# Laying the feature map's weights out once, so that the fusing products read contiguous columns

## The chip, the cores and the metric

The kernel runs on one core of a Trainium2 chip. The metric is the device time of one execution in microseconds (us). Three executions of the kernel before took 780.72, 781.41 and 781.92 us; their median is 781.41 us.

## What is computed

Two attention branches share the input x (2048 tokens of 512 values) and are mixed by a gate. Branch A is softmax attention, branch B is linear attention with a learned feature map. Both have 32 heads of 16 values. Cut to what matters:

```python
# A
q, k, v = split_heads(x @ A_wqkv)
a = softmax(q @ k.T * 16 ** -0.5) @ v                 # per head
a = merge_heads(a) @ A_wo
# B
q, k, v = split_heads(x @ B_wqkv)
pq, pk = q @ w_phi[h], k @ w_phi[h]                   # per head, 16 x 16
phi = lambda p: concat(softmax(p), softmax(-p))
kv, z = phi(pk).T @ v, phi(pk).sum(tokens)
b = merge_heads((phi(pq) @ kv) / (phi(pq) @ z + 1e-6)) @ B_wo
g = sigmoid((x * gate_w).sum(-1))
out = g * a + (1 - g) * b
```

## The kernel before

**Branch A** fills most of the span. It runs over 4 chunks of 512 queries, 8 groups of heads in each, and 16 tiles of 128 keys, with 4 heads of a group side by side in the TensorE array. `_scores` (L993) multiplies kT and qT for one head: 32 rows of the array, 128 columns, 512 queries. ScalarE takes most of the scores, two banks of PSUM at a time, and writes their exponentials to ET (`_exp`, L1041). VectorE takes the others (L900, L925) and builds approximate exponentials from integer bits in the tiles vs and va. `_values` (L1100) multiplies the exponentials with V or with its scaled copy V2, on 32 columns of the array per head. V2 is written by GpSimd, one copy for each pair of key tiles (L805). `_norm` divides by the sums.

**Branch B** is threaded through the same time. `_b_fuse` (L1205 to L1224) folds the feature map into the projection: WT holds the transposed B_wqkv for the keys (s=1) or the queries (s=0), and the products of WT with w_phi (L1216) give new projection weights, which VectorE copies to WB (L1221). There are 4 column chunks of WT by 4 groups of 8 heads for each s, so 32 products of 128 x 128 by 128 columns; four of them share a bank of PSUM. For each group of 8 heads, the tile wphi holds a 128 x 128 matrix that is zero but for eight 16 x 16 blocks on its diagonal. Its columns stand in the order of heads and, in each head, of features. The rest of branch B wants the order (group of four heads, feature, head in the group), so each product reads its moving operand through a rearranged view:

```python
ins = e.matmul(self._bank(job)[:, P * cp:P * cp + P], self.WT[:, cp, P * c:P * c + P],
               self.wphi[:, cp, :].rearrange("p (g i f) -> p g f i", g=2, i=4), start=True, stop=True)
```

The fused weights are used in `_b_pair`, the values in `_b_v`, and the two meet in `_b_kv` (L1356) and `_b_num` (L1406). The gate's products with x are computed by TensorE too, between the two rounds of fusing.

**Loads.** `_consts` sets wphi to zero on GpSimd (L611) and loads w_phi into it with eight DMAs on SyncE's queue (L615). WT is loaded transposed (L1208), for s=1 early, for s=0 when the products of s=1 have been read.

**Order of the work.** All operations are recorded first with engine, estimated cost, buffers read and written, and a priority. `Plan.order` then picks one after another in simulated time and so fixes the order on each engine; `Plan.emit` writes the engines' instruction streams with waits on semaphores. On each engine, instructions run in that order. The recorded cost of four fusing products is 4 * c_pe(128), whatever the view.

Of the kernel before, what the change touches and what calls it, by code (L numbers as in the profile page):

```python
# [7 lines left out]
ALU = mybir.AluOpType  # L8
# [5 lines left out]
DH = 16  # L14
# [51 lines left out]
class Plan:  # L66
# [43 lines left out]
    def op(self, eng, fn, cost, reads=(), writes=(), deps=(), name="", prio=0.0, rel=-99, kind="full",  # L110
           acquire=None, release=None, lat=None, array=None, strips=None, also=None):
        o = Op(eng, fn, cost, name, prio, rel, kind, self.LAT[eng] if lat is None else lat)
        found = {}
        for b in reads:
            for w in b.writers:
                found[id(w)] = w
        for b in writes:
            for w in b.readers or b.writers:
                found[id(w)] = w
            if b.readers:  # L120
                for w in b.writers:
                    found[id(w)] = w
        for d in deps:
            if d is not None:
                found[id(d)] = d
        found.pop(id(o), None)
        o.deps = list(found.values())
        for b in reads:
            b.readers.append(o)
        for b in writes:  # L130
            b.writers, b.readers = [o], []
        o.acquire, o.release, o.also = acquire, release, also
        o.strips = strips
        o.port = eng == "POOL" or eng == "DVE" and name in self.PORT
        o.held = eng == "PE" and acquire is None and name in self.HOLDING
        o.array = cost if array is None else array
        self.ops.append(o)
        return o
# [257 lines left out]
class _Kernel:  # L396
# [183 lines left out]
    def _consts(self):  # L580
        op = self.plan.op
        B = Buf
        self.b_iden, self.b_mask = B(), B()
        self.b_V = [[B() for _ in range(self.NT // 2)] for _ in range(4)]
        self.b_V2 = [[B() for _ in range(self.NT // 2)] for _ in range(4)]
        self.early = {}
        self.b_VB = [B() for _ in range(4)]
        op("POOL", lambda e: e.memset(self.iden[:], 0.0), 0.25, writes=[self.b_iden], prio=-90)
        op("POOL", lambda e: e.affine_select(
            out=self.iden[:], in_=self.iden[:], pattern=[[-1, P]], compare_op=ALU.not_equal,  # L590
            fill=1.0, base=0, channel_multiplier=1), 0.3, reads=[self.b_iden], writes=[self.b_iden], prio=-89)
        for s in range(2):
            op("DVE", lambda e, s=s: e.tensor_reduce(
                self.mask[:, s:s + 1], self.iden[:].rearrange("p (i s d) -> p s i d", i=4, s=2)[:, s], AX.XY, ALU.add),
                0.3, reads=[self.b_iden], writes=[self.b_mask] if s else [B()], prio=-80)
        self.b_bm = B()
        op("DVE", lambda e: e.tensor_reduce(self.bm[:], self.iden[:].rearrange("p (v i) -> p i v", i=4), AX.X, ALU.add),
           0.3, reads=[self.b_iden], writes=[self.b_bm], prio=-20)
        n = 4 * self.NT * self.VCP
        self.o_vones = op("POOL", lambda e: e.memset(  # L600
            self.V[:, 0:n].rearrange("p (h v) -> p h v", v=17)[:, :, 16:17], 1.0), 1.0, prio=-70)
        self.o_vpad = op("POOL", lambda e: e.memset(self.V[:, n:], 0.0), 0.1, prio=-69)
        self.o_vbones = op("POOL", lambda e: e.memset(self.VB[:, :, :, 64:68], 1.0), 0.3, prio=-20)
        self.b_zero, self.b_warm = B(), B()
        op("DVE", lambda e: e.memset(self.warm[:], 1.0), 0.3, writes=[self.b_warm], prio=-95)
        op("POOL", lambda e: e.memset(self.zero[:], 0.0), 0.1, writes=[self.b_zero], prio=-75)
        self.b_guess = [B(), B(), B()]
        for t, b in zip((self.guess, self.guess_n, self.guess_b), self.b_guess):
            op("POOL", lambda e, t=t: e.memset(t[:], 0.0), 0.2, writes=[b], prio=-10)
        self.b_wphi0 = B()  # L610
        z = op("POOL", lambda e: e.memset(self.wphi[:], 0.0), 0.6, prio=-30)  # L611
        parts = []
        phi = self.B_w_phi.rearrange("(c h) d f -> h d c f", h=8)
        for hh in range(8):
            parts.append(lambda e, hh=hh: e.dma_start(self.wphi[16 * hh:16 * hh + 16, :, 16 * hh:16 * hh + 16], phi[hh]))  # L615
        self._shared_dma("wphi", parts, self.b_wphi, -5, [z])
        self.dma("SP", "wob", lambda e: e.dma_start(self.WoB[:], self.B_wo.rearrange("(q p) n -> p q n", p=P)),
                 writes=[self.b_WoB], prio=-3, lat=4.5)

# [539 lines left out]
    def _branch_b(self):  # L1159
        op, NT, NQC = self.plan.op, self.NT, self.NQC  # L1160
        B = Buf
        self.b_bq = [B() for _ in range(self.NBQ)]
        self.b_WT = B()
        self.b_WP = [B() for _ in range(2)]
        self.b_tree, self.b_bsum, self.b_brec = B(), B(), B()
        self.b_kv = [B() for _ in range(2)]
        self.b_kvbd, self.b_onB, self.b_rinvB = B(), [B(), B()], [B(), B()]
        self.b_numB, self.b_numR = [B(), B()], B()
        self.b_eps = [B() for _ in range(4)]
        self.b_phiT = [B() for _ in range(4)]  # L1170
        for x in self.b_phiT:
            x.readers = [r for s in (1, 2) for b in self.b_WA[s] for r in b.readers]
        self.b_onTB = [B() for _ in range(4)]
        self.outs = []
        self.n_pair = self.n_phit = 0
        z = op("POOL", lambda e: e.memset(self.kvbd[:], 0.0), 1.0, writes=[self.b_kvbd], prio=-10)
        for s in (1, 0):
            self._b_fuse(s, self.K0 - 10 + 5 * (1 - s))
        for b in self.b_onTB:
            b.readers = list(self.b_WT.readers)  # L1180
        for t in range(0, NT, 2):
            due = self.K0 + self.SK * t
            if self.RATIO:
                slot = self._b_pair(1, t, due)
                for k in range(2):
                    self._b_v(t + k, due + self.BV + k)
                self._b_kv(t, slot, due + self.BV + 7)
                continue
            self._b_v(t, due)
            self._b_v(t + 1, due + 1)  # L1190
            self._b_kv(t, self._b_pair(1, t, due), due + 12)
        self._b_kvbd(self.Q0 - 2)
        for ch in range(NQC):
            for tt in (0, 2):
                t = 4 * ch + tt
                due = self.Q0 + self.SQ * t
                phi = self._b_pair(0, t, due)
                for k in range(2):
                    self._b_phit(tt + k, phi, k, due + 12 + 2 * k)
                    self._b_num(t + k, self._num_due(t + k))  # L1200
                    self._b_out(tt + k)
# [4 lines left out]
    def _b_fuse(self, s, due):  # L1206
        op = self.plan.op
        self.dma("SP", f"wt{s}", lambda e: e.dma_start(self.WT[:], self.B_wqkv[:, D * s:D * s + D], transpose=True),  # L1208
                 writes=[self.b_WT], prio=-8 if s else due - 10, rel=-99 if s else due - 12, lat=5.0, cost=8.0 if s else 4.4)
        done = []  # L1210
        for c in range(4):
            job = Job()

            def mm(e, c=c, job=job):
                for cp in range(4):
                    ins = e.matmul(self._bank(job)[:, P * cp:P * cp + P], self.WT[:, cp, P * c:P * c + P],  # L1216
                                   self.wphi[:, cp, :].rearrange("p (g i f) -> p g f i", g=2, i=4), start=True, stop=True)
                return ins
            m = op("PE", mm, 4 * self.c_pe(128), reads=[self.b_WT, self.b_wphi], name="wphi", prio=due + 1,
                   acquire=job)  # L1220
            done.append(op("DVE", lambda e, c=c, job=job: e.tensor_copy(  # L1221
                self.WB[:, c, D * s:D * s + D], self._bank(job)), self.c_dve(512), deps=[m],
                name="wphi_ev", prio=due + 1, release=job))
        self.b_WP[s].writers = done  # L1224
# [329 lines left out]
```

## Time and profile before

| | |
|---|---|
| median of 3 executions | 781.41 us |
| profiled execution, time | 781.93 us |
| profiled execution, span | 780.1 us |
| busy: TensorE (PE), VectorE (DVE), ScalarE (ACT), GpSimd (POOL) | 754.9, 711.2, 753.0, 208.9 us |
| exponentials, L1041 on ACT | 785, 725.3 us |
| idle time of ACT before them | 13.4 us, 13.0 of it ended by the scores of L993 |
| fusing products, L1216 on PE | 32, 7.8 us, between 56.8 and 89.6 us |
| mean granted TensorE clock | 0.986 |

The profile shows one execution; its span lies within the time of the same execution. The engines are PE (matmul), PEld (loading of weights into the array), DVE, ACT and POOL. Line numbers are those of the kernel before. "Busy" on PE counts matmuls in flight, which overlap: a matmul's own duration is longer than the distance between the starts of two that follow each other. "<-" names what ended an idle time, and the clock column is the share of full speed that TensorE was granted.

### The profile page before, as it was taken

The page shows a single profiled execution, that of the slowest core. Times are in us where ns is not written, and L with a number is a line of the kernel's source. Part 1 is how long each engine was busy: PE and PEld are TensorE (multiplying, and loading weights), DVE is VectorE, ACT ScalarE, POOL GpSimd, SP SyncE. Part 2 cuts the span into 40 slices and gives each one's busy share as a digit, 9 for nine tenths or more (in the row PEclk, how much of TensorE's full clock was granted, in tenths as well). Part 3 has the DMA queues.
Part 4 walks back from the last instruction along what each step waited for, and adds up shares of the span by engine and source line. Part 5 has one row for each costly group of instructions (what it writes and reads, how often), then busy time and mean ns, then how long its engine had stood idle before and what let it go on. Part 6 is the DMA issues. An engine that isn't in the chain of part 4 may idle for free.

```text
span 780.1 us, 16892 instructions
## 1 busy us (share of the span) xinstructions
PE 754.9 (97%) x7047; PEld 218.5 (28%) x7111; DVE 711.2 (91%) x1158; ACT 753.0 (97%) x807; POOL 208.9 (27%) x300
## 2 busy tenths in 40 slices
PE   8999999999999999999999999999999999999998
PEld 3322223322222222222222222222222222222222
DVE  3864898899999999999998999999999999999994
ACT  6996899999999999999999999999999999999996
POOL 2210034601533234414234132130424231140000
PEclk9995999999999999999999999999999999999999
DMA  9501010000000000010111103112020312102010
GB/s 221 131 2 28 1 14 5 12 1 8 9 1 9 8 4 12 2 14 2 15 36 43 27 21 35 35 32 26 15 42 14 40 30 49 21 8 35 15 16 28
DMA packets 89180, 20.78 MB, mean 27 GB/s; under 512 B 83472, under 2 KB 88592, under 8 KB 89104
## 3 DMA queue, kind: packets, MB, share of 16 engines
q1 hardware_dynamic: 87232, 18.92, 13.5%
q8 instruction: 56, 0.92, 0.5%
q10 hardware_dynamic: 1872, 0.79, 0.4%
q14 instruction: 20, 0.16, 0.1%
HBM read 4.21 MB, written 2.10 MB: 8 GB/s over the span
## 4 chain that ended last, share of the span: by engine, by line
ACT 74%; PE 19%; DVE 5%; DMA 1%; issue 1%
ACT ET L1041 71%; PE ps L993 6%; PE ps L1100 5%; PE ps L677 4%; ACT bq L1283 3%; PE ps L788 2%; DVE vs L900 2%; DVE vs L925 1%; PE ps L1216 1%; DMA xT<-in_A_x_dram 1%; DVE bq L1256 0%; DVE btree L1277 0%; DVE ghB L841 0%; PE ps L685 0%; PE ps L724 0%
## 5 line engine op out<-in xcount | busy, mean ns | idle before, releaser
L1041 ACT ACTIVATE ET<-ps 128x1024 bf16<-128x1024 f32 (+1 forms) x785 | 725.3, 1165 | 13.4 <-PE ps L993 13.0
L900 DVE TENSOR_SCALAR vs<-ps 128x512 uint16<-128x512 f32 x482 | 312.5, 682 | 25.0 <-PE ps L993 23.5
L993 PE MATMUL ps<-qT,kT 32*128 32x512 bf16 (+1 forms) x2052 | 317.2, 387 | 10.9 <-ACT ET L1041 5.9
L925 DVE TENSOR_SCALAR vs<-vs 128x2048 uint16<-128x2048 uint16 (+2 forms) x242 | 233.8, 976 | 1.2
L1100 PE MATMUL ps<-vs,V 128*32 128x512 bf16 x1928 | 211.3, 385 | 0.6 <-DVE vs L925 0.3
L1100 PE MATMUL ps<-ET,V 128*32 128x512 bf16 x1566 | 196.6, 390 | 0.3 <-DVE vs L900 0.2
L993 PEld LDWEIGHTS ps<-qT,kT 32*128 32x128 bf16 x2052 | 77.7, 91 | 317.7 <-ACT ET L1041 291.5
L1286 POOL TENSOR_TENSOR btree<-btree 128x512 f16<-128x512 f16 (+1 forms) x32 | 37.7, 1180 | 187.5 <-DVE btree L1285 186.5
L1100 PEld LDWEIGHTS ps<-ET,V 128*32 128x32 bf16 x1566 | 49.1, 94 | 82.4 <-issue 73.5
L1107 PE MATMUL ps<-kT,zero 128*32 128x512 bf16 x664 | 66.5, 384 | 0.0
L1100 PEld LDWEIGHTS ps<-vs,V 128*32 128x32 bf16 x1928 | 48.2, 95 | 51.2 <-issue 31.1
L1274 POOL TENSOR_SCALAR bq<-bq 128x1024 bf16<-128x1024 bf16 x16 | 20.3, 1266 | 138.3 <-DVE bq L1256 94.5
L677 PE MATMUL ps<-WB,xT 128*128 128x512 bf16 x169 | 51.9, 383 | 2.7 <-issue 2.2
L1138 POOL TENSOR_TENSOR T<-T,rinv 128x512 bf16<-128x512 f32 x15 | 17.3, 1156 | 109.4 <-DVE rinv L1136 109.4
L767 POOL TENSOR_SCALAR qT<-qtmp,mask 128x512 bf16<-128x512 bf16 x30 | 25.8, 866 | 45.3 <-DVE qtmp L762 44.9
L677 PE MATMUL ps<-xT,WA 128*128 128x512 bf16 x95 | 32.9, 401 | 2.5 <-issue 1.6
L1121 DVE STREAM_TRANSPOSE T<-ps 128x512 f32<-128x512 f32 x32 | 22.7, 710 | 13.1 <-PE ps L1100 13.0
L1283 ACT ACTIVATE bq<-bq 128x2048 bf16<-128x2048 bf16 x16 | 32.9, 2056 | 0.0
L1256 DVE CAST bq<-ps 128x512 bf16<-128x512 f32 x32 | 21.7, 681 | 1.7 <-PE ps L677 1.7
L1107 PEld LDWEIGHTS ps<-kT,zero 128*32 128x32 bf16 x664 | 15.9, 94 | 19.3 <-issue 17.5
L805 POOL TENSOR_SCALAR V<-V 128x544 bf16<-128x544 bf16 x16 | 12.7, 793 | 30.3 <-DVE V L798 30.1
L1280 DVE TENSOR_TENSOR bq<-bq,btree 128x2048 bf16<-128x2048 bf16 x16 | 19.5, 1220 | 0.1
(86 smaller groups left out, 414.1 us busy)
## 6 DMA issues: line engine op xcount, KB each, us to landing
T<-T SPq DMA_DIRECT2D x240, 8.0 KB, 1.8
WB<-in_B_wqkv_dram SPq DMA_DIRECT2D x1, 1536.0 KB, 7.1
out_dram<-WB SPq DMA_DIRECT2D x12, 128.0 KB, 1.7
WA<-in_A_wqkv_dram SPq DMA_DIRECT2D x2, 384.0 KB, 5.0
WoB<-in_B_wo_dram SPq DMA_DIRECT2D x1, 512.0 KB, 3.8
WoA<-in_A_wo_dram SPq DMA_DIRECT2D x1, 512.0 KB, 4.8
WA<-in_A_wqkv_dram ACTq DMA_DIRECT2D x2, 128.0 KB, 3.5
WA<-in_A_wqkv_dram ACTq DMA_DIRECT2D x1, 256.0 KB, 5.0
```

Source lines behind the costliest of these rows:

```text
L677: return e.matmul(out, lhs, rhs, start=start, stop=stop)
L767: x = self.plan.op("POOL", lambda e, side=side: e.tensor_scalar(self.qT[:, s0 + side, :], tmp, self.mask[:, side:side + 1], 0.0, op0=ALU.m ...
L900: bits = lambda e, to, src: e.tensor_scalar(to, src, SCALE * LOG2E * 128.0, float(ORIGIN), op0=ALU.mult, op1=ALU.add)
L925: o = op("DVE", lambda e, k=k, src=src, dst=dst: e.tensor_scalar(dst, src, float(STEPS[k - 1]), None, op0=ALU.add), 0.16 + k * n * QCH * 0 ...
L993: return e.matmul(out[:, cols], self.kT[32 * i:32 * i + 32, cp, kt * TOK:(kt + 1) * TOK], self.qT[32 * i:32 * i + 32, s, cols], start=True ...
L1041: o = plan.op("ACT", lambda e: e.activation(self.ET[:, a % NS:a % NS + n, cols], self.ps[:, a % NR:a % NR + n, cols], ACT.Exp, scale=SCALE ...
L1100: ins = e.matmul(self._bank(ot)[32 * i:32 * i + 32, :], v[:, v0:v0 + 32], tile, start=(kt == 0), stop=(kt == self.NT - 1), tile_position=( ...
L1107: ins = e.matmul(self._bank(ot)[32 * i:32 * i + 32, :], self.zero[:], self.kT[:, 0, 0:QCH], start=False, stop=False, tile_position=(0, 32 ...
L1121: t1 = op("DVE", lambda e: e.transpose(T1[:, side].rearrange("p b s -> p (b s)"), src()), 0.735, deps=last, writes=[b_T1[side]], name="n_t ...
L1256: [lambda e, b, k=k: e.tensor_copy(bq[:, k].rearrange("p (g s v) -> p g s v", g=8, s=2)[:, :, 0, :], b.rearrange("p (g v) -> p g v", g=8))],
L1283: op("ACT", lambda e: e.activation(flat, flat, ACT.Exp), 1.789, reads=[b], writes=[b], name="b_exp", prio=due + 1)
L1286: + [("b_sum", two(128 * n), lambda e, n=n: e.tensor_tensor(half[:, :, 0:n], half[:, :, 0:n], half[:, :, n:2 * n], ALU.add), (n <= self.P_ ...
```

## The change

The zeroed tile with the loads of w_phi is now the first half of onB, a tile that branch B uses late. One GpSimd instruction copies it into wphi with the columns in the order that the products want. The products read wphi as it lies. The copy reads the buffer b_wphi0 and writes b_wphi; b_wphi0 also becomes the buffer record of onB's first half, so the planner keeps the later writes to onB behind the copy.

```diff
@@ _consts
         self.b_wphi0 = B()
-        z = op("POOL", lambda e: e.memset(self.wphi[:], 0.0), 0.6, prio=-30)
+        raw = self.onB[:, 0, :]
+        z = op("POOL", lambda e: e.memset(raw, 0.0), 0.6, prio=-30)
         parts = []
         phi = self.B_w_phi.rearrange("(c h) d f -> h d c f", h=8)
         for hh in range(8):
-            parts.append(lambda e, hh=hh: e.dma_start(self.wphi[16 * hh:16 * hh + 16, :, 16 * hh:16 * hh + 16], phi[hh]))
-        self._shared_dma("wphi", parts, self.b_wphi, -5, [z])
+            parts.append(lambda e, hh=hh: e.dma_start(
+                raw.rearrange("p (c j) -> p c j", c=4)[16 * hh:16 * hh + 16, :, 16 * hh:16 * hh + 16], phi[hh]))
+        self._shared_dma("wphi", parts, self.b_wphi0, -5, [z])
+        op("POOL", lambda e: e.tensor_scalar(
+            self.wphi[:].rearrange("p c (g f i) -> p (c g) f i", f=DH, i=4),
+            raw.rearrange("p (g i f) -> p g f i", i=4, f=DH), 1.0, 0.0, op0=ALU.mult, op1=ALU.add), 0.8,
+           reads=[self.b_wphi0], writes=[self.b_wphi], name="wphi_p", prio=5)
@@ _branch_b
-        self.b_kvbd, self.b_onB, self.b_rinvB = B(), [B(), B()], [B(), B()]
+        self.b_kvbd, self.b_onB, self.b_rinvB = B(), [self.b_wphi0, B()], [B(), B()]
@@ _b_fuse
                     ins = e.matmul(self._bank(job)[:, P * cp:P * cp + P], self.WT[:, cp, P * c:P * c + P],
-                                   self.wphi[:, cp, :].rearrange("p (g i f) -> p g f i", g=2, i=4), start=True, stop=True)
+                                   self.wphi[:, cp, :], start=True, stop=True)
```

## The prediction

> **What bounds the kernel now.** First the page: its slices of the span and the first line of its chain.
>
> ```profile
> PE   8999999999999999999999999999999999999998
> ...
> ACT  6996899999999999999999999999999999999996
> ...
> PEclk9995999999999999999999999999999999999999
> ...
> ACT 74%; PE 19%; DVE 5%; DMA 1%; issue 1%
> ```
>
> ScalarE (ACT) is full in every slice but the first, the last, and slices 3 and 4 counted from 0 (58.5 to 97.5 us); in slice 3 the TensorE clock is at half. The exponentials of L1041 (785 of them, 725 of the 780 us) set the end, so a microsecond counts where ACT stood idle. Next, ACT's timeline (start, length of the run of instructions, idle time before it and who ended it):
>
> ```profile
> 14.94 43.25 ACT L1041 ACTIVATE ET<-ps 128x1024 bf16<-128x1024 f32 x47 [0.45 <-PE ps L993]
> 58.57 1.94 ACT L1041 ACTIVATE ET<-ps 128x1024 bf16<-128x1024 f32 x2 [0.39 <-PE ps L993]
> 62.40 2.11 ACT L1041 ACTIVATE ET<-ps 128x1024 bf16<-128x1024 f32 x2 [1.89 <-PE ps L993]
> ...
> 79.39 1.02 ACT L1041 ACTIVATE ET<-ps 128x1024 bf16<-128x1024 f32 x1 [0.32 <-PE ps L993]
> ...
> 84.16 5.62 ACT L1041 ACTIVATE ET<-ps 128x1024 bf16<-128x1024 f32 x6 [1.15 <-PE ps L993]
> 90.22 5.60 ACT L1041 ACTIVATE ET<-ps 128x1024 bf16<-128x1024 f32 x6 [0.44 <-PE ps L993]
> ```
>
> For 43 us ACT runs without a gap. From 58 to 90 us it waits again and again for the scores of L993, so here PE sets the pace. After 112 us that timeline shows one idle of 0.17 us until the last exponential. So what is won between 58 and 90 us should reach the end whole. What PE did there, by stretches of 3.41 us laid at the clock's changes (length; PE, PEld, DVE, ACT, POOL busy with counts; clock; DMA share; GB/s):
>
> ```profile
> 55.15:58.57 3.42, 3.26 (x30) 1.03 (x23) 3.04 (x6) 3.04 (x4) 0.00 (x0) 1.00 0.00 0
> 58.57:61.98 3.41, 3.41 (x20) 1.44 (x16) 3.09 (x6) 1.94 (x2) 0.00 (x0) 1.00 0.00 0
> 61.98:65.39 3.41, 3.41 (x16) 0.66 (x15) 2.49 (x3) 2.32 (x3) 0.00 (x0) 0.50 0.64 136
> ...
> 75.63:79.05 3.42, 3.42 (x23) 0.59 (x22) 0.98 (x2) 2.45 (x3) 0.00 (x0) 0.50 0.00 0
> 79.05:82.46 3.41, 3.25 (x24) 1.20 (x24) 2.17 (x4) 2.54 (x4) 0.00 (x0) 1.00 0.00 0
> ```
>
> The clock is 0.50 in five such stretches, 61.98 to 79.05 us. The stretch before them holds only 20 PE instructions, 12 of them fusing products. Last, the products beside contiguous ones, from PE's timeline:
>
> ```profile
> 59.12 2.80 PE L1216 MATMUL ps<-wphi,WT 128*128 128x128 bf16 x12
> ...
> 143.08 2.36 PE L788 MATMUL ps<-WA,xT 128*128 128x256 bf16 x20
> ...
> 154.47 0.42 PE L1356 MATMUL ps<-VB,bq 128*128 128x68 bf16 x8
> ```
>
> A product lasts 0.397 us (the line's own rows, median), so twelve in 2.80 us start every (2.80-0.397)/11 = 0.218 us. The contiguous ones of 256 columns (mean 0.277 us) start every (2.36-0.277)/19 = 0.110 us, those of 68 columns (mean 0.195 us) every (0.42-0.195)/7 = 0.032 us. A product of 128 columns thus costs twice one of 256, and about as much as 512 columns would. What sets it apart is its moving operand: in the trace's records its pattern is [4,16,2], neighbours 16 elements apart.
>
> **The change, part by part.**
>
> *PE's products, contiguous.* The price of 128 contiguous columns lies between the rows of 68 and 256 columns, 0.032 and 0.110 us; in proportion to columns 0.032+0.078*60/188 = 0.057 us. I take it. The 32 products save 32*(0.218-0.057) = 5.2 us of PE (3.5 at 0.110). The Trainium skill, "TensorE: Matmul & The Clock Gate", section "Back-to-back issue gap", prices a warm matmul by its columns alone, N/2.4+2.5 ns, 56 ns for 128, and does not mention the moving operand's stride. By that alone the products would already be fast and the sum would be 0; the row of 0.218 us disagrees.
>
> *The clock.* I weigh a stretch by columns streamed times the quarter of the array that they use (scores of L993 and values of L1100 use a quarter). 58.57 to 61.98: 4 scores and 12 products, 4*128+12*128 = 2,048 full columns, at the 0.43 ns of L788's spacing 0.88 us, 0.26 of the stretch. The least that kept the clock at 1.00: 0.35 (79.05 to 82.46: 5 scores, 10 values, 7 products) and 0.37 (707.1 to 710.5). So the slow products starve the stretch and the clock falls after it. With the products contiguous the same instructions from 58.57 to 85.87 us (some 9.9 us by this measure) fall into some 16.2 us, 0.61 on average, like the rest (median 0.60). So I take it that the clock stays up. Against this: at 10.8 us it fell after a stretch of 0.42, with PE idle for 0.64 us in it; the share is not the whole rule. The Trainium skill, same page, section "What's actually happening", lets the clock drop after an idle window and rise after one sustained busy window of some 3.4 us. By that, a PE 3.41 of 3.41 us busy would not have dropped, and busy again would be up after one window, not five; the half clock would then not be the products' doing, and the sum would be 5.0 us, the products' own part below. The trace disagrees in both.
>
> *What ACT gains.* An exponential lasts 1.02 us alone; in the runs without a gap they start every (43.25-1.02)/46 = 0.92 us, and again (5.62-1.02)/5 = 0.92. The first run ends at 58.19, so its last start is 57.17.
> - 57.17 to 62.40, 3 intervals: 5.23-2.76 = 2.5 us lost to the first 16 products.
> - 62.40 to 79.39, 11 intervals: 16.99-10.12 = 6.9 us lost to the half clock.
> - 79.39 to 84.16, 3 intervals: 4.77-2.76 = 2.0 us lost to the next 12 products.
> - 84.16 to 90.22, 6 intervals: 6.06-5.52 = 0.5 us lost to the last four.
>
> Together 11.9 us, the ceiling. Can PE keep up? Its passes from 61.98 to 79.05 are 8.4 us at full clock, against 10.1 us of exponentials; yes. What is late next: DVE. From 56.85 to 64.5 it is nearly full, and its cast of L749, at 67.16 behind 2.66 us of idle time, is now due 6 intervals after 57.17, at 62.7: up to 1.8 us late, less the one exponential (0.92) by which scores run ahead. Elsewhere, with DVE full (101 to 106 us), ACT idles 1.48 us. Between 0 and 1.5 us of new idle time I take 0.8, the middle. Saving 11.1 us.
>
> *GpSimd's new copy.* The order of instructions on PE, DVE, ACT and SP is unchanged; PE's first product loses only its direct wait for the load. GpSimd gets one instruction between the fifth and sixth copies to V2 (L805):
>
> ```profile
> 29.00 0.65 POOL L805 TENSOR_SCALAR V<-V 128x544 bf16<-128x544 bf16 x1 [1.81 <-DVE V L798]
> 34.12 1.55 POOL L805 TENSOR_SCALAR V<-V 128x544 bf16<-128x544 bf16 x1 [4.48 <-DVE V L798]
> ```
>
> It waits for the eight loads (last issued at 27.1, 1.6 to 3.4 us to landing: 28.7 to 30.5), so it starts between 29.65 and 30.5. Its length is between 0.65 (this row) and 2.28 us (L600, the 512-element memset with a stride); I take 1.2. It ends by 32.8, inside the 4.48 us of idle time that hide it. Behind it queue the last three V2 copies; uncovered, each further microsecond would hold these, then PE's products on V2. Cost 0. Its reader, the product at 56.85, is 24 us away. The memset of another tile (0.78 us) and the eight loads only change their target, and that tile's own first values come at 405.6 us (L1427): 0.
>
> *Sum.* Profiled execution: span 780.1, time 781.93; less 11.1 gives 770.8. It lies 0.5 us above the median of 781.41, from which the sum is 770.3. Between the two I say **770.6**.
>
> **Rivals.**
> 1. *The clock falls once all the same*, here or later. For: 10.8 us. Then one episode's 6.9 us stays, and only 5.0 us (2.5+2.0+0.5) go: 781.4-5.0 = 776.4, or 776.9 from the profiled execution. 12%.
> 2. *The layout was not the reason*, the products stay at 0.218 us: 781.4. Against: both contiguous neighbours. 3%.
> 3. *Slower.* All later work moves 11.1 us against the clock's 3.41 us stretches, and thin ones (0.37 at 707 us, 0.39 at 406.7) drop below what the clock bears, between 0.26 and 0.35. Each episode costs 6.9 us; it decides from the second: 781.4-11.1+13.8 = 784.1. For: nothing measures that bound exactly. Against: after 79 us the clock stays at 1.00 to the last 2 us, and four executions lie between 780.7 and 781.9 us. 3%.
>
> **The numbers.** My forecast holds 82%, its own range 768.8 (the ceiling, and half of the 1.48 us gone as well) to 773.0 (2.4 us of new idle time more than taken). To leave out under 2 in 10 the range takes in rival 1: 768.8 to 777.0. A measurement here tells some 0.2% (1.6 us) from no change: faster 0.94, within 0.03, slower 0.03.
>
> **What would show it.** The products at 0.2 to 0.25 us each and spaced 0.06; slice 3 of the clock at 9; ACT's idle before L1041 down from 13.4 to about 4 us; the copy inside 29 to 34 us; DVE's busy time unchanged. Wrong if the clock still reads 0.50 after the first products, or if ACT still waits for L993 at full clock.

## The result, and the profile after

The changed kernel takes **768.64 us** in the median (4 executions, 768.03 to 769.98), beside 781.56 us for the kernel before (4 executions): ratio 0.9835, 95% interval 0.9809 to 0.9861. Forecast were 770.6 us and a range of 768.8 to 777.0; the result is 2.0 us faster than forecast and 0.2 us below the range. The profiled execution: time 769.25, span 767.3 us. Line numbers after L611 are now 6 higher (the exponentials are L1047, the scores L999, the products L1222).

The page's slices and the first line of its chain:

```profile
ACT  6999999999999999999999999999999999999996
...
PEclk9999999999999999999999999999999999999999
...
ACT 75%; PE 19%; DVE 6%; issue 1%
```

Slices 3 and 4 of ACT are full, and slice 3 of the clock reads 9. ACT's timeline (start, length, instruction, count, idle time before and who ended it):

```profile
14.53 68.91 ACT L1047 ACTIVATE ET<-ps 128x1024 bf16<-128x1024 f32 x75 [0.41 <-PE ps L999]
83.15 0.48 ACT L839 ACTIVATE gh<-gh 128x128 f32<-128x128 f32 x1
83.35 8.65 ACT L1047 ACTIVATE ET<-ps 128x1024 bf16<-128x1024 f32 x9
93.27 4.69 ACT L1047 ACTIVATE ET<-ps 128x1024 bf16<-128x1024 f32 x5 [1.27 <-PE ps L999]
```

The sixteen idle times of before between 58 and 102 us are gone; the gate's exponential (before at 95.67) comes at 83.15. Of these waits only the one of 1.27 us remains (1.28 before). All of ACT's idle time before exponentials went from 13.4 to 3.1 us. The products on PE, and GpSimd's copy:

```profile
58.15 0.84 PE L1222 MATMUL ps<-wphi,WT 128*128 128x128 bf16 x12
```

```profile
29.31 1.09 POOL L619 TENSOR_SCALAR wphi<-onB 128x512 bf16<-128x512 bf16 x1
33.71 1.55 POOL L811 TENSOR_SCALAR V<-V 128x544 bf16<-128x544 bf16 x1 [3.31 <-DVE V L804]
```

A product lasts 0.219 us (median of the line) and starts every (0.84-0.219)/11 = 0.056 us. The copy takes 1.09 us, and 3.31 us of idle time are left behind it.

### The profile page after: what moved, and what is told of

It reads as the page before. It is cut to its first block, busy times and chain, and to the rows that moved or that the text cites. A ratio compares the mean times of both kernels' runs of the same rounds, so it can differ in the third digit from the quotient of the medians.

```text
span 767.3 us, 16893 instructions
## 1 busy us (share of the span) xinstructions
PE 742.6 (97%) x7047; PEld 216.9 (28%) x7111; DVE 710.1 (93%) x1158; ACT 751.0 (98%) x807; POOL 209.1 (27%) x301
## 4 chain that ended last, share of the span: by engine, by line
ACT 75%; PE 19%; DVE 6%; issue 1%
ACT ET L1047 72%; PE ps L999 6%; PE ps L1106 5%; PE ps L683 4%; ACT bq L1289 3%; PE ps L794 2%; DVE vs L906 2%; DVE vs L931 1%; PE ps L674 1%; DVE bq L1262 0%; PE ps L1222 0%; DVE btree L1283 0%; DVE ghB L847 0%; PE ps L691 0%; DVE T L1127 0%
## 5 line engine op out<-in xcount | busy, mean ns | idle before, releaser
L1047 ACT ACTIVATE ET<-ps 128x1024 bf16<-128x1024 f32 (+1 forms) x785 | 723.3, 1172 | 3.1 <-PE ps L999 2.8
L999 PE MATMUL ps<-qT,kT 32*128 32x512 bf16 (+1 forms) x2052 | 314.9, 385 | 11.0 <-ACT ET L1047 5.8
L999 PEld LDWEIGHTS ps<-qT,kT 32*128 32x128 bf16 x2052 | 77.7, 91 | 312.9 <-ACT ET L1047 297.0
L1127 DVE STREAM_TRANSPOSE T<-ps 128x512 f32<-128x512 f32 x32 | 22.7, 708 | 12.0 <-PE ps L1106 11.9
L683 PEld LDWEIGHTS ps<-WB,xT 128*128 128x128 bf16 x192 | 12.9, 97 | 23.6 <-issue 18.8
```

The costliest lines, as they stand in the source:

```text
L683: return e.matmul(out, lhs, rhs, start=start, stop=stop)
L999: return e.matmul(out[:, cols], self.kT[32 * i:32 * i + 32, cp, kt * TOK:(kt + 1) * TOK], self.qT[32 * i:32 * i + 32, s, cols], start=True ...
L1047: o = plan.op("ACT", lambda e: e.activation(self.ET[:, a % NS:a % NS + n, cols], self.ps[:, a % NR:a % NR + n, cols], ACT.Exp, scale=SCALE ...
L1127: t1 = op("DVE", lambda e: e.transpose(T1[:, side].rearrange("p b s -> p (b s)"), src()), 0.735, deps=last, writes=[b_T1[side]], name="n_t ...
```

## The experiments

The theory: strided columns hold PE four times as long (some 5 us in all), and twelve of them in a row leave the array so empty that the clock falls (some 7 us more). Rivals: the clock falls because PE is held, or because it reads with a stride, or for a reason outside the products. Medians, each with its ratio to the kernel before on the same chip (each edit moves the line numbers a little):

| kernel | us | ratio (95% interval) |
|---|---|---|
| s1_strided | 778.82 | 0.9960 (0.9936 to 0.9983) |
| s0_strided | 770.85 | 0.9858 (0.9828 to 0.9887) |
| full4 | 773.53 | 0.9900 (0.9869 to 0.9931) |
| thin | 779.23 | 0.9956 (0.9924 to 0.9988) |
| copy_only | 781.30 | 0.9997 (0.9976 to 1.0019) |
| after2, after3 (the changed kernel) | 768.54, 768.87 | 0.9841 (0.9809 to 0.9873), 0.9837 (0.9799 to 0.9876) |
| strided_fill | 776.00 | 0.9932 (0.9899 to 0.9964) |
| price | 808.05 | 1.0339 (1.0311 to 1.0368) |

**One round strided.** The changed kernel, with the old view of the copy's source in one round (`s == 1` or `s == 0`):

```diff
+w = self.onB[:, 0, P * cp:P * cp + P].rearrange("p (g i f) -> p g f i", g=2, i=4) if s == 1 else self.wphi[:, cp, :]
 ins = e.matmul(self._bank(job)[:, P * cp:P * cp + P], self.WT[:, cp, P * c:P * c + P],
-               self.wphi[:, cp, :], start=True, stop=True)
+               w, start=True, stop=True)
```

> The changed kernel, but its first 16 products (keys, s=1) read the old strided order again, from the tile that the copy reads; the last 16 stay contiguous. My theory (the slow products of s=1 lose 2.5 us themselves, and starve TensorE's array so that the clock falls): the half clock is back from 62 us for about five stretches, 768.6+2.5+6.9 = 778.0 us. Rival (the clock fell for another reason, and only the products' own time counts): clock 1.00, 768.6+2.5 = 771.1 us.

> The changed kernel, but its last 16 products (queries, s=0) read the old strided order again. My theory: eight in a row beside scores and values leave the stretch at 0.35 of the array, as before the change, so the clock stays 1.00; 768.6+2.5 = 771.1 us. Rival (any round of strided products brings the clock down, whatever else is in the stretch): half clock after about 74 us, 778 us.

Measured: 778.82 us with the first round strided (forecast 778.0), 770.85 with the second (771.1). ACT's timeline in s1_strided:

```profile
61.57 1.94 ACT L1047 ACTIVATE ET<-ps 128x1024 bf16<-128x1024 f32 x2 [1.76 <-PE ps L999]
...
73.75 1.02 ACT L1047 ACTIVATE ET<-ps 128x1024 bf16<-128x1024 f32 x1 [0.91 <-PE ps L999]
...
79.59 13.10 ACT L1047 ACTIVATE ET<-ps 128x1024 bf16<-128x1024 f32 x14 [0.27 <-PE ps L999]
```

and in s0_strided:

```profile
8.41 61.12 ACT L1047 ACTIVATE ET<-ps 128x512 bf16<-128x512 f32 x68 [0.85 <-PE ps L999]
69.70 2.10 ACT L1047 ACTIVATE ET<-ps 128x1024 bf16<-128x1024 f32 x2 [0.17 <-PE ps L999]
72.95 5.62 ACT L1047 ACTIVATE ET<-ps 128x1024 bf16<-128x1024 f32 x6 [1.15 <-PE ps L999]
```

In the first the half clock is back for five stretches (62.14 to 79.21 us in the trace's clock records), and the second round runs without a gap. In the second the clock stays at 1.00, and the idle times of 1.15 and 0.44 us of before are back beside one of 0.17. The mean clock says the same of the other executions: 0.985 to 0.988 in the twelve of s1_strided, 0.997 to 1.000 in the five of s0_strided. So twelve strided products in a row bring the clock down, and eight do not. That 778.82 came so near 778.0 is in part luck: the 6.9 us in the sum are those of one execution of before, and they vary (see the part on the clock below).

**The same hold, full array and empty array.**

```diff
@@ full4
+for _ in range(4):
     ins = e.matmul(self._bank(job)[:, P * cp:P * cp + P], self.WT[:, cp, P * c:P * c + P],
                    self.wphi[:, cp, :], start=True, stop=True)
@@ thin, behind each four products
+for _ in range(3):
+    ins = e.matmul(self._bank(job)[0:32, :], self.zero[0:32, :], self.kT[0:32, 0, 0:QCH], start=False,
+                   stop=False, tile_position=(0, 0), skip_group_check=True)
```

> The changed kernel with every contiguous product issued four times into the same place (values unchanged): TensorE is held as long as by the strided ones (4*0.056 = 0.22 us), but the array is full all the while. My theory (array use sets the clock): clock 1.00, only the products' own time returns, 768.6+5.0 = 773.6 us. Rival (the long hold itself, whatever streams in it, brings the clock down or makes the stage late): half clock for about five stretches, 780.5 us.

> The changed kernel with three passes of 512 columns on a 32 x 32 corner of the array behind each four contiguous products, adding zeros (values unchanged): TensorE is held about as long as by the strided products, it streams at full rate, but uses 1/16 of the array. My theory (array use sets the clock): the clock falls to 0.50 again after the first round, about 780.5 us. Rival (reading with a stride brings the clock down, or the clock follows TensorE being busy): clock 1.00, 773.6 us.

Measured: full4 773.53 us, as forecast (773.6). On PE its 48 products last about as long as the twelve strided ones (2.85 and 2.80 us); one long wait on ACT follows, and no half clock. PE's products, the stretch that holds their first part (length; PE, PEld, DVE, ACT, POOL busy; clock; DMA share; GB/s), and ACT:

```profile
57.48 2.85 PE L1223 MATMUL ps<-wphi,WT 128*128 128x128 bf16 x48
```

```profile
54.85:58.26 3.41, 3.41 (x46) 2.17 (x46) 2.99 (x5) 2.99 (x4) 0.00 (x0) 1.00 0.00 0
```

```profile
60.70 11.11 ACT L1047 ACTIVATE ET<-ps 128x1024 bf16<-128x1024 f32 x12 [1.82 <-PE ps L999]
```

So the hold alone costs 773.53-768.54 = 5.0 us, and holding PE does not bring the clock down (mean clock 0.996 to 1.000 in its six executions). In thin the stretch of the passes and the next one read:

```profile
56.68:60.09 3.41, 3.41 (x27) 1.36 (x23) 3.02 (x4) 1.87 (x2) 0.00 (x0) 1.00 0.00 0
60.09:63.50 3.41, 2.94 (x16) 0.63 (x15) 2.53 (x4) 2.05 (x2) 0.00 (x0) 0.50 0.45 99
```

PE is busy for all of 3.41 us, nothing reads with a stride, and the clock falls. So a low use of the array is enough. The stretch holds 2 scores, 12 products and 9 of the passes, 2,080 full columns or 0.26 by the prediction's measure. Without the part of the array that they use, the columns do not fit: thin streams 7,168 in this stretch, and the clock falls; after2 streams 5,632 between 6.91 and 10.32 us, and it stays. Nor is it that the passes add zeros. The kernel's own filling passes (L1107) multiply by a tile of zeros too, and in this stretch of before they are 0.52 of 0.71, all else being 0.19:

```profile
591.05:594.46 3.41, 3.19 (x48) 1.16 (x44) 3.41 (x6) 3.41 (x5) 0.65 (x1) 1.00 0.02 5
```

The clock stays there and after it. In thin the clock did not fall in every execution. Of the twelve, seven at a mean clock of 0.980 to 0.993 took 778.8 to 787.5 us, five at 0.996 to 1.000 took 774.3 to 776.9 us. The latter are near the rival's 773.6, the former about the theory's 780.5; the median, 779.23, lies between.

**The copy alone.** The changed kernel with the view above in both rounds (`if True`).

> The changed kernel with GpSimd's copy made as in the change, but with all 32 products reading the old strided order from the copy's source. My theory (the copy is hidden in GpSimd's idle time, all of the gain is the products'): as the kernel before on the same chip, within 1 us, with half clock from 62 us. Rival (the other tile or the copy's place does part of the gain or the harm): off by more than 2 us.

Measured: no difference from the kernel before (ratio 0.9997), with the half clock from 62.05 us. The copy and the other tile neither gain nor cost.

**More work for the old layout.** The kernel before, with one line ahead of each four products:

```diff
+e.matmul(self._bank(job), self.WT[:, 0, P * c:P * c + P], self.kT[:, 0, 0:QCH], start=True, stop=True)
 for cp in range(4):
```

> The kernel before, with its strided products, and one useless pass of 512 contiguous columns through the whole array ahead of each four of them (the products overwrite its result, values unchanged). TensorE has 8*0.215 = 1.7 us more to do, and the stretch with twelve products rises from 0.26 to about 0.45 of the array. My theory (array use sets the clock): the clock stays at 1.00 and more work makes the kernel faster, 768.5+5.0 = 773.5 to 775.5 us. Rival (TensorE's hold is what costs): the half clock stays and the extra passes come on top, 781.9+1.7 = 783.6 us.

Measured: 776.00 us, 0.7% less than the kernel before with more for PE to do, and 0.5 us above the range expected. But the clock did not hold every time. Eight of the twelve executions had a mean clock of 0.996 to 1.000; the three at 1.000 took 774.4 to 774.6 us. Four had 0.978 to 0.991 and took 780.3 to 788.1 us, the profiled one (780.28 us) among them. In it the clock fell at 61.25 us for four stretches:

```profile
57.84:61.25 3.41, 3.41 (x17) 1.51 (x15) 2.53 (x4) 1.16 (x2) 0.00 (x0) 1.00 0.00 0
61.25:64.66 3.41, 3.41 (x17) 0.66 (x15) 2.36 (x3) 2.58 (x3) 0.00 (x0) 0.50 0.69 146
```

The stretch before that drop holds 2 scores, 12 products and 2 of the passes, 2*128+12*128+2*512 = 2,816 full columns, 0.35 of the array by the prediction's measure: as many as in the stretch from 79.05 us of before, which kept the clock, and not the 0.45 expected. Two early stretches of 3,328 full columns (0.42) went either way as well: the clock fell after that from 7.37 us of before and stayed after that from 6.91 us of after2. So the measure is not exact, and the bound not sharp.

**The plan told the truth.** The kernel before, with the products' true hold in the plan:

```diff
-m = op("PE", mm, 4 * self.c_pe(128), reads=[self.b_WT, self.b_wphi], name="wphi", prio=due + 1,
-       acquire=job)
+m = op("PE", mm, 4 * 0.22, reads=[self.b_WT, self.b_wphi], name="wphi", prio=due + 1,
+       acquire=job, array=4 * self.c_pe(128))
```

> The kernel before, with its strided products, but the plan is told their true hold (0.22 us each in place of 0.056) and their small use of the array, so it may order other work and filling passes around them; the whole later order moves too. My theory: the hold itself stays, the clock mostly stays up, 773 to 777 us, behind the changed kernel. Rival (the layout is the only remedy): as the kernel before, 781 to 783 us.

Measured: 808.05 us, far from both. ACT's timeline, and the products' line (count, durations in ns, first and last start):

```profile
73.22 89.58 ACT L1041 ACTIVATE ET<-ps 128x1024 bf16<-128x1024 f32 x97
178.62 1.91 ACT L1283 ACTIVATE bq<-bq 128x2048 bf16<-128x2048 bf16 x1 [15.83 <-DVE bq L1280]
199.92 1.91 ACT L1283 ACTIVATE bq<-bq 128x2048 bf16<-128x2048 bf16 x1 [19.38 <-DVE bq L1280]
```

```profile
L1216 PE MATMUL ps<-wphi,WT x32: 377/397/397, 162.6 to 183.4; 128*128 128x128 bf16 x32
```

Up to 162 us ACT runs almost without a gap and the clock stays at 1.00, but no fusing product has run by then: the new order moves all 32 to between 162.6 and 183.4 us. There the clock falls at 163.83 us, after the first four. From 162.8 to 201.7 us ACT has no exponential of branch A at all; it waits 35 us for VectorE ahead of two of branch B's (L1283). So the products are not hidden behind other work but stand in the open. The expectation left out what else a changed price moves. The run shows how much of this plan depends on one number; it does not measure the layout.

**The step between columns.** The changed kernel, each four products with another view (shortened; one execution, 771.98 us):

```diff
+v = lambda k: self.wphi[:, cp, :].rearrange("p (n k) -> p k n", k=k)   # k = 1, 2, 4, 8 | 16, 32, 64, old
```

> The changed kernel, where each group of four products reads the same tile with another step between neighbouring columns: 1, 2, 4 and 8 elements in the first round, 16, 32, 64 and the old pattern (16) in the second. The columns come in a wrong order, so branch B's values are wrong and the time of the products is the only thing to read. My theory has no rule for the size of the step; from the two rows (0.056 us at 1, 0.22 us at 16) either every step over 1 costs 0.22 us a product, or the price grows with the step, to 0.22 us at 16, and then stays there.

PE's timeline, steps of 2, 4, 8, then 16, 32, 64 elements:

```profile
57.92 0.40 PE L1227 MATMUL ps<-wphi,WT 128*128 128x128 bf16 x4
58.16 0.62 PE L1229 MATMUL ps<-wphi,WT 128*128 128x128 bf16 x4
58.60 1.09 PE L1231 MATMUL ps<-wphi,WT 128*128 128x128 bf16 x4
69.98 1.09 PE L1233 MATMUL ps<-wphi,WT 128*128 128x128 bf16 x4 [0.16 <-issue]
72.40 1.03 PE L1235 MATMUL ps<-wphi,WT 128*128 128x128 bf16 x4
73.25 0.67 PE L1237 MATMUL ps<-wphi,WT 128*128 128x128 bf16 x4
```

Single products last 0.219, 0.295, 0.407, 0.412, 0.393 and 0.285 us (medians), so they start every 0.06, 0.11, 0.23, 0.23, 0.21 and 0.13 us; contiguous ones took 0.06. A step of 2 is free, 4 costs double, 8 to 32 about fourfold, which neither expectation had: the price is full at 8 already, and falls again behind 32. The step of 64, where columns alternate between two places, costs only double; why was not tried.

**The changed kernel again**, for its spread:

> The changed kernel itself once more, for its spread and for the half clock near 10 us. My theory: its times split by whether the clock falls once at the start (some 1 us more where it does), 768 to 770 us; no half clock in the fusing stage in any run. Rival: an execution with a half clock in the fusing stage, near 775 us.

> The changed kernel beside the filled one on the same chip, and some more of its executions, for the one in ten that took 773.7 us at a mean clock of 0.991. My theory: 767.8 to 770 us, with single executions of a half clock (some 5 us more) at most in one of ten. Rival (the changed kernel is free of it): all within 767.8 to 770 us.

Measured: 768.54 and 768.87 us. Of the 16 executions of the changed kernel, 15 lie between 767.8 and 771.4 us. One, of after2, took 773.67 us at a mean clock of 0.991. It was not the profiled one, so where its clock fell stays open. With it after2 missed its 768 to 770 us, and after3, with one execution of 771.37, its 767.8 to 770. The half clock near 10 us comes and goes: in the profile of the result it is there (10.32 to 13.74 us), in that of after2 it is not, and the gate's exponential is at 82.22 in place of 83.15 us, though ACT's first exponential starts at 8.56 in place of 8.20. That makes it worth some 1.3 us.

## Why the prediction was right, and where it missed

*What bounds the kernel, and where.* Right. The gain was made between 57 and 96 us of before and reached the end whole: the gate's exponential comes 12.5 us earlier, the last copy on ACT 12.8 us.

*The price of a product.* Forecast 0.057 us, measured 0.056; own part 5.0 us, measured 5.0 (full4). The rule by columns alone (the Trainium skill, "TensorE: Matmul & The Clock Gate", section "Back-to-back issue gap") gives 0.056 us too. The same section of the Trainium skill means it for a matmul by itself and puts those of a stream, with 128 columns each and weight loads between, at some 81 ns. The products have a weight load each and still start every 0.056 us. So the rule holds for contiguous columns and for a step of 2; from 8 to 32 elements it is low by about a factor of four, as the trace of before said.

*The clock.* Right in mechanism: s1_strided, thin and full4 part array use from stride and from hold. The 6.9 us are one execution's. The spread of the kernel before shows that they vary: in its 57 later executions it took, among others, 775.3 to 775.7 us at a mean clock of 0.995, 779.9 to 780.3 at 0.989, 781.2 to 781.9 at 0.986 and 785.0 to 785.8 at 0.978. That is 10 us for 0.017*780 = 13 us of clock, with nothing else changed; most likely the half clock is longer in some and shorter in others, but of the kernel before only one execution has a trace. By copy_only and full4 the clock's part is 781.3-773.5 = 7.8 us in the median.

*New idle time: the step that failed.* The sum gave back 0.8 us, the middle of 0 to 1.5; 0 came. It took VectorE as full until 64.5 us and its cast of kT as up to 1.8 us late. But VectorE had itself waited for the products (idle times of 0.39 and 0.19 us ended by L1216 in the trace of before). Afterwards it takes the same work in one piece, and the cast starts at 63.02 us, 6.3 us after the exponential at 14.53+46*0.917 = 56.7, where 6 intervals (5.5 us) had it due. So it is 0.8 us late and inside the one exponential (0.92 us) of lead. VectorE before:

```profile
57.92 0.69 DVE L1221 CAST WB<-ps 128x512 bf16<-128x512 f32 x1 [0.39 <-PE ps L1216]
61.95 0.69 DVE L1221 CAST WB<-ps 128x512 bf16<-128x512 f32 x1 [0.19 <-PE ps L1216]
67.16 0.69 DVE L749 CAST kT<-ps 128x512 bf16<-128x512 f32 x1 [2.66 <-PE ps L993]
```

and after:

```profile
63.02 0.68 DVE L755 CAST kT<-ps 128x512 bf16<-128x512 f32 x1
```

*The rest of the 2.0 us.* In the profiled executions the first long run on ACT begins at 14.53 in place of 14.94, ahead of all products; its 0.4 us are not the change's. Together with the 0.8 above, with 0.2 by which the ceiling was too small (12.1 us in the stage, not 11.9) and 0.2 won later on, that is the distance of 12.7 measured (781.93-769.25) from 11.1; the other 0.4 us to the median come from the executions' spread. The range's low end held only idle time; the half clock near 10 us, worth some 1.3 us where it does not come, was in none of its terms.

*GpSimd's copy.* Right: 1.09 us (1.2 forecast), hidden, cost 0.

*Rivals.* The first (the clock falls all the same) was seen at most once in 16 executions, at 773.67 us where 776.4 was forecast. The second is out (0.056 us a product). The third did not come. Its counter-evidence was weak, though: four executions within 1.2 us looked like a steady kernel, and the 57 later ones spread over 10 us.

## What to carry to other kernels

Price a matmul by how it reads its moving operand, not by its columns alone: look for one that lasts longer than a wider neighbour. Where PE sets the pace for a while, look at the granted clock just after it; a few slow instructions can cost more through a half clock behind them than by themselves. And where a stage is freed, idle times of other engines inside it that the same instructions caused are freed as well.

## What the runs showed of the hardware

The step between columns that is free is small (strides): 2 elements of 2 bytes; with 4 elements 128 columns cost 0.11 us, with 8 elements 0.23 us. The Trainium skill, "SBUF — State Buffer", section "Door 1: The DMA port swizzle", puts the free step at 8 such elements; the runs disagree.

The clock follows how much of the array is used, and PE being busy does not keep it: it fell with PE busy 3.41 of 3.41 us, at 0.26 of the array (before, thin), and stayed through the same hold with the array full (full4). Passes over zeros count as use (before, 591.05 us). The half clock then lasted four stretches of 3.41 us (thin, strided_fill) or five (before, s1_strided, copy_only), where the one near 10 us lasts one. What ends it was not tested. By columns streamed the bound is not sharp: the clock fell after some stretches of 0.35 and 0.42 of the array and stayed after others.
